# Value products of an attention in two halves of the head's dimension, on 64x32 instead of 64x64 tiles of the TensorE array

## Chip, cores and metric

The kernel runs on one core of one Trainium2 chip. The metric is the device time of one execution in microseconds (us). Three runs of the kernel before gave 911.26, 908.46 and 911.06 us; the median is 911.06 us. A measurement of this kernel can tell a difference from no change when it is over about 0.3%, which is 2.7 us.

## The reference

The reference is an attention followed by a feed-forward block, all in float32. For 8 batches and 8 heads of 576 positions with a head dimension of 64:

```python
scores = scale * np.matmul(q, k.transpose(0, 1, 3, 2))
rel = pos[:, None] - pos[None, :]
mask_plain = (rel >= 0) & (rel < 32)
mask_dil = (rel >= 0) & (rel < 128) & (rel % 4 == 0)
...
attn = np.exp(scores - np.max(scores, axis=-1, keepdims=True))
attn = attn / (np.sum(attn, axis=-1, keepdims=True) + 1e-09)
out = np.matmul(attn, v)
...
h = x @ w_in
sp = np.maximum(h, 0.0) + np.log1p(np.exp(-np.abs(h)))
y = (h * erf(sp)) @ w_out
```

Heads 0 to 3 use the plain mask, heads 4 to 7 the dilated one. `x` is the attention's output as a matrix of 4608 tokens by 512, `w_in` is 512x2048 and `w_out` 2048x512. The last matrix `y` is the result.

## The kernel before, in words

**The attention** works on units. The sequence is cut into strips of 32 queries (`STRIP`), and each strip looks at 64 keys (`KEYS`): its own 32 and the 32 before it. The dilated heads are put in an order in which the same holds. A unit is 8 strips (`SPU`) of two heads; there are 72 units (`NU`). A unit goes through these steps:

- `scores` (L221): 16 products on TensorE, for each strip and each of the two heads `h`. The stationary operand is 64 partitions (the head's dimension) by 32 queries, the moving one 64 partitions by 64 keys. Each runs on a tile of the array of 64 rows by 32 columns, at row 0 or 64 and at column 0, 32, 64 or 96, so that eight such tiles lie beside each other.
- `mask_max` on VectorE, `exponents` on ScalarE, `normalize` on VectorE and GpSimd.
- `transposes` (L260): two transposes of 128x128 on TensorE, and a copy `turned` (L264) of the result from PSUM into `pT`, which holds keys on partitions.
- `values` (L279): 16 products on TensorE, for each of 4 columns of strips `s`, the two halves `p` of the partitions and the two heads `h`. The stationary operand is the value tile `v`, 64 keys by the 64 of the head's dimension; the moving one is 64 keys by 32 queries of `pT`. Each runs on a tile of 64 rows by 64 columns, of which there are four. The result, 64 partitions by 32, lies in PSUM.
- `rows` (L321): ScalarE copies that PSUM out into a tile of rows, which later becomes the input of the feed-forward block.

The operands are plain float32, and such a product is carried out as two pairs of a weight load and a matmul. So the 1152 products of `values` show as 2304 weight loads and 2304 matmuls in the trace, and so do the 1152 of `scores`.

**The feed-forward block** splits its operands into a high and a low part and multiplies them in three products of 128x128 tiles (`mm1`, L528, `mm1_fast`, L649, and `mm2`, L702). These fill TensorE for most of the span.

**The order of the work** is written out by hand. The first 14 units are scored in `first_visit`, one visit each; in each visit from the fourth on, the unit of three visits before is transposed and gets its value products, with a few idle products (`busy`, L361) between. After that, a loop over half steps `x` of the feed-forward block takes up further visits at half steps that `visits` lists. In such a visit `attend` issues the value products of the units that are ready, and right behind them, on the same queue of TensorE, the scores of the units that are due:

```python
def attend(ready, scored):
    for u in ready:
        values(u)
    for u in scored:
        scores(u)
    for u in ready:
        rows(u)
```

Ten visits have one unit in each list. From then on a visit has two: 24 visits have two ready and two scored units, and the last two visits have only value products, of two units and of one. With the 11 visits of the beginning that makes 11 + 10 + 48 + 2 + 1 = 72 units.

The value products of a unit wait for its copied transposes and for the DMA that brought `v`; the scores wait for the DMA that brought `qk`.

Of the kernel before, what the change touches and what calls it, by code (L numbers as in the profile page):

```python
# [18 lines left out]
P = 128  # L19
B, H, S, D = 8, 8, 576, 64  # L20
# [5 lines left out]
STRIP = 32  # L26
NSTRIP = S // STRIP
KEYS = STRIP + WIN
# [111 lines left out]
def attn_moe_kernel(ctx: ExitStack, tc: tile.TileContext, qk, v, masks, eye, w_in, w_out, out):  # L140
    nc = tc.nc
# [43 lines left out]
    def place(u, p):  # L185


        if u < FREE:
            return acc[(u + 1 + 2 * p) % 4][:, p * P:(p + 1) * P]
        at = PARTS * P + (u in second) * P  # L190
        return spb[p][:, at:at + P]
# [80 lines left out]
    def values(u):  # L272
        vt, pt = vz[u % 2], pz[u in second]
        for s in range(SIDE):
            qs = slice(s * STRIP, (s + 1) * STRIP)
            for p in range(PARTS):
                ks, xp = slice(p * KEYS, (p + 1) * KEYS), place(u, p)
                for h in range(2):
                    nc.tensor.matmul(xp[h * D:(h + 1) * D, qs], vt[ks, s, h, :],  # L279
                                     pt[ks, h * P + s * STRIP:h * P + (s + 1) * STRIP], start=True, stop=True,  # L280
                                     tile_position=(p * KEYS, h * D))

    def attend(ready, scored):
        for u in ready:
# [5 lines that stand above are left out]
# [73 lines left out]
    def first_visit(n):  # L363

        m = n - LAG
        copy = nc.scalar.copy if n in EARLY else nc.vector.tensor_copy
        if has(m):
            transposes(m)
        scores(n)
        if n != DEEP - 3:  # L370
            load_qk(n + 3 if n < DEEP - 3 else n + 2)
        if n < 3:
            load_w(n)
        busy(2 if has(m) else 3)
        if has(m):
            turned(m, copy)
        if n in EARLY:
            prep_act()
        if has(m):
            values(m)  # L380
            busy(2)
        if has(n - 2):
            normalize(n - 2)
        mask_max(n)
        part_lo()
        if has(m):
            rows(m)
            finish(m)
        if m == NBLK - 1:
            part_lo()  # L390
        exponents(n)
        load_v(n - 1)
# [80 lines left out]
    h = ps.tile([P, TOK], F32, name="h")  # L473
# [3 lines left out]
    at = {0: [[x[:, i, 0:TOK] for x in xs] for i in range(2)]}  # L477
# [456 lines left out]
```

## Time and profile before

| | |
|---|---|
| median of three runs | 911.06 us (908.46 to 911.26) |
| span of the profiled execution (the page gives no other time of it) | 908.9 us |
| TensorE matmuls busy | 884.3 us, 97% of the span |
| weight loads busy | 753.5 us, 83% |
| VectorE, ScalarE, GpSimd busy | 669.6, 600.7 and 77.9 us |
| mean granted TensorE clock | 0.994 |
| chain of work that ended last | 85% TensorE, of it L279 and L221 about 3% each |

In the rows, PE is TensorE's matmul and PEld its weight load, which overlaps it; DVE is VectorE, ACT ScalarE, POOL GpSimd and SP SyncE. L279 is line 279 of the kernel before. A row of the timeline gives the start and the length of a merged group in us, from its first start to its last end, and its count. In a line's own view stand the shortest, median and longest duration of one instruction in ns, and the first and the last start in us. Matmuls are pipelined: many are under way at once, so the pace is read from their starts and not from their lengths.

### The profile page before, as it was taken

How to read it: one execution, taken by the hardware profiler on the slowest of the kernel's cores; microseconds unless marked ns; L12 is line 12 of the kernel's file. 1: busy time of each engine (PE TensorE's matmuls, PEld its weight loads, DVE VectorE, ACT ScalarE, POOL GpSimd, SP SyncE). 2: the span in 40 equal slices, each digit the busy share in tenths (PEclk: the TensorE clock that was granted, in tenths of full speed). 3: DMA queues.
4: the chain of work that ended last, by engine and by line, in shares of the span. 5: the costliest groups of instructions: out<-in, count | busy, mean ns of one | idle time of the engine just before them, and what ended most of it. 6: DMA issues, size and time to landing. Idle time of an engine off the chain costs nothing.

```text
span 908.9 us, 22857 instructions
## 1 busy us (share of the span) xinstructions
PE 884.3 (97%) x9129; PEld 753.5 (83%) x9129; DVE 669.6 (74%) x1702; ACT 600.7 (66%) x1267; POOL 77.9 (9%) x97
## 2 busy tenths in 40 slices
PE   7789999999999999999999999999999999999998
PEld 3367777888887888889989988888988999999996
DVE  3889879886688888668776777678666866776555
ACT  5889879876678687666776676669654644545442
POOL 2322100000011100000100000000000000000000
PEclk7999999999999999999999999999999999999999
DMA  8784444432458688687668765877567546655521
GB/s 276 250 273 149 137 159 135 136 127 80 150 199 324 232 284 309 241 284 227 219 206 283 262 213 191 289 266 252 185 237 230 185 146 230 233 180 203 199 84 47
DMA packets 69450, 188.89 MB, mean 208 GB/s; under 512 B 9184, under 2 KB 17632, under 8 KB 63200
## 3 DMA queue, kind: packets, MB, share of 16 engines
q1 hardware_dynamic: 69056, 186.91, 60.9%
q8 instruction: 72, 1.18, 0.5%
q10 hardware_dynamic: 288, 0.52, 0.1%
q14 instruction: 34, 0.28, 0.1%
HBM read 153.85 MB, written 33.55 MB: 206 GB/s over the span
## 4 chain that ended last, share of the span: by engine, by line
PE 85%; DVE 7%; DMA 3%; ACT 2%; issue 1%; POOL 1%; SPq 0%; DVEq 0%; POOLq 0%; ACTq 0%
PE acc L702 40%; PE h L649 15%; PE tx L649 12%; PE h L528 10%; PE sp L279 3%; PE sp L221 3%; PE sp L260 1%; DMA dbl<-in_w_in_dram 1%; DMA v<-in_v_dram 1%; DVE s L684 1%; DVE hc L670 1%; DVE w L465 1%; ACT prob L242 1%; DVE prob L232 1%; POOL prob L255 0%
## 5 line engine op out<-in xcount | busy, mean ns | idle before, releaser
L702 PE MATMUL acc<-wout_hi,ghi 128*128 128x512 f32 x576 | 228.4, 397 | 0.5 <-DVE ghi L687 0.4
L702 PE MATMUL acc<-wout_lo,ghi 128*128 128x512 f32 x576 | 225.7, 392 | 0.0
L674 ACT ACTIVATE s<-hc 128x1024 f32<-128x1024 f32 x72 | 76.5, 1062 | 189.4 <-DVE hc L663 171.2
L702 PE MATMUL acc<-wout_hi,glo 128*128 128x512 f32 x576 | 159.0, 389 | 0.0
L702 PEld LDWEIGHTS acc<-wout_hi,glo 128*128 128x128 f32 x576 | 108.1, 188 | 22.7
L702 PEld LDWEIGHTS acc<-wout_hi,ghi 128*128 128x128 f32 x576 | 108.6, 188 | 20.7 <-DVE ghi L687 0.9
L702 PEld LDWEIGHTS acc<-wout_lo,ghi 128*128 128x128 f32 x576 | 108.7, 189 | 19.5
L255 POOL TENSOR_TENSOR prob<-prob,rinv 128x256 f32<-128x256 f32 x72 | 69.0, 968 | 539.0 <-DVE ssum L253 314.1
L688 DVE TENSOR_TENSOR glo<-s,ghi 128x512 fp32r<-128x512 f32 x144 | 100.1, 695 | 5.5 <-PE acc L702 0.5
L242 ACT ACTIVATE prob<-prob,nmax 128x64 f32<-128x64 f32 x288 | 96.4, 338 | 7.6 <-DVE nmax L232 7.1
L684 DVE TENSOR_TENSOR s<-hc,s 128x1024 f32<-128x1024 f32 x72 | 92.9, 1290 | 9.2 <-ACT s L677 9.1
L528 PE MATMUL h<-x,win 128*128 128x512 f32 x384 | 96.6, 394 | 2.6 <-DVE hc L670 2.5
L649 PE MATMUL h<-win 128*128 128x256 f32 x720 | 98.1, 283 | 0.0
L674 ACT ACT_TABLE_LOAD x72 | 92.4, 1283 | 1.3
L677 ACT ACT_TABLE_LOAD x72 | 92.4, 1283 | 1.3
L649 PEld LDWEIGHTS h<-win 128*128 128x128 f32 x720 | 91.6, 192 | 0.0
L528 PEld LDWEIGHTS h<-x,win 128*128 128x128 f32 x384 | 71.2, 188 | 18.8 <-DVE hc L670 3.7
L677 ACT ACTIVATE s<-s 128x1024 f32<-128x1024 f32 x72 | 76.3, 1060 | 0.8
L232 DVE CUSTOM_DVE_ANT_0 prob<-sp,cst 128x64 f32<-128x64 f32 x288 | 45.4, 220 | 36.9 <-ACT rows L321 20.1
L687 DVE CAST ghi<-s 128x512 fp32r<-128x512 f32 x144 | 68.5, 475 | 3.1 <-PE acc L702 0.6
L321 ACT COPY rows<-sp 128x128 f32<-128x128 f32 (+7 forms) x167 | 27.9, 308 | 57.3 <-PE sp L221 55.0
L659 DVE TENSOR_TENSOR hc<-h,hc 128x512 f32<-128x512 f32 x48 | 33.2, 692 | 41.1 <-PE h L649 40.8
(110 smaller groups left out, 1257.6 us busy)
## 6 DMA issues: line engine op xcount, KB each, us to landing
win<-ws SPq DMA_DIRECT2D x48, 1024.0 KB, 5.5
win<-ws SPq DMA_DIRECT2D x48, 768.0 KB, 4.5
v<-in_v_dram SPq DMA_DIRECT2D x72, 256.0 KB, 4.1
qk<-in_qk_dram SPq DMA_DIRECT2D x45, 272.0 KB, 3.9
dbl<-in_w_in_dram SPq DMA_DIRECT2D x16, 512.0 KB, 4.0
dbl<-in_w_out_dram SPq DMA_DIRECT2D x16, 512.0 KB, 3.7
ws<-x SPq DMA_DIRECT2D x32, 256.0 KB, 4.1
xT<-rows SPq DMA_DIRECT2D x24, 288.0 KB, 5.0
```

The lines of the kernel that those rows point to most:

```text
L232: nc.vector.tensor_tensor_reduce(out=pr[:, g, :], in0=sps[h][:, u % 2, p, :], in1=mask[QUADS.index(kinds(u, p))], scale=-SCALE, scalar=BIG ...
L242: nc.scalar.activation(out=probs[u][:, j, :], in_=probs[u][:, j, :], func=AF.Exp, scale=-1.0, bias=nmax[:, j:j + 1], accum_out=sums[u][:, ...
L255: nc.gpsimd.tensor_tensor(probs[u], probs[u], rinv.broadcast_to([P, 2 * PARTS, KEYS]), op=ALU.mult)
L528: nc.tensor.matmul(h, win_at[:, ftp, j, cc // 2, w, cc % 2, :], x[cc], start=(k == 0 and i == 0), stop=(k == CC - 1 and i == 2))
L649: nc.tensor.matmul((h, bank)[b][:, half * HN:(half + 1) * HN], w[:, k, wi, c, :], x[:, xi, c, :], start=(c == 0 and n == 0), stop=(c == 1 ...
L659: nc.vector.tensor_tensor(out=a[:, 0:2], in0=x, in1=a[:, 2:3].broadcast_to([P, 2, HN]), op=ALU.add)
L674: nc.scalar.activation(out=ls[t], in_=hs[t], func=AF.Softplus)
L677: nc.scalar.activation(out=ls[t], in_=ls[t], func=AF.Erf)
L684: nc.vector.tensor_tensor(out=e, in0=hc, in1=e, op=ALU.mult)
L687: nc.vector.tensor_copy(out=ghi, in_=e[:, j])
L688: nc.vector.tensor_tensor(out=glo, in0=e[:, j], in1=ghi.bitcast(F32), op=ALU.subtract)
L702: nc.tensor.matmul(acc[tt], g[:, tt * P:(tt + 1) * P], w[:, ft, :], start=(first and w is wout_hi and g is ghi), stop=(last and g is glo))
```

## The change

Each value product of 64 keys by 64 of the head's dimension becomes two products of 64 keys by 32, one for each half of the dimension. Each half has the same moving operand as the whole had. Its tile of the array has 64 rows and 32 columns, and its result goes to the same 32 partitions of the same place in PSUM as that half of the result did before.

```diff
                 for h in range(2):
-                    nc.tensor.matmul(xp[h * D:(h + 1) * D, qs], vt[ks, s, h, :],
-                                     pt[ks, h * P + s * STRIP:h * P + (s + 1) * STRIP], start=True, stop=True,
-                                     tile_position=(p * KEYS, h * D))
+                    for d in range(0, D, STRIP):
+                        at = h * D + d
+                        nc.tensor.matmul(xp[at:at + STRIP, qs], vt[ks, s, h, d:d + STRIP],
+                                         pt[ks, h * P + s * STRIP:h * P + (s + 1) * STRIP], start=True, stop=True,
+                                         tile_position=(p * KEYS, at))
```

`values` now issues 32 products per unit instead of 16, or 64 pairs of a weight load and a matmul instead of 32. All else stays, the waits too. On TensorE's queue, this is the end of the first unit's value products and the beginning of the second's, and the beginning of the scores, in a visit of two units, before (`sp_90` and `sp_91` are the two PSUM banks, one for each half of the rows; `x2` counts equal neighbours; 64x32 is the result's shape):

```order
L279 MATMUL sp_90<-pT_88,v_87 64x32 x2
L279 MATMUL sp_91<-pT_88,v_87 64x32 x2
L279 MATMUL sp_90<-pT_89,v_86 64x32 [waits DMAHW1_49]
L279 MATMUL sp_90<-pT_89,v_86 64x32
...
L279 MATMUL sp_91<-pT_89,v_86 64x32 x2
L221 MATMUL sp_90<-qk_83 32x64 [waits DMAHW6_49]
L221 MATMUL sp_91<-qk_83 32x64
```

And the same place now:

```order
L281 MATMUL sp_90<-pT_88,v_87 32x32 x4
L281 MATMUL sp_91<-pT_88,v_87 32x32 x4
L281 MATMUL sp_90<-pT_89,v_86 32x32 [waits DMAHW1_49]
L281 MATMUL sp_90<-pT_89,v_86 32x32 x3
...
L281 MATMUL sp_91<-pT_89,v_86 32x32 x4
L221 MATMUL sp_90<-qk_83 32x64 [waits DMAHW6_49]
L221 MATMUL sp_91<-qk_83 32x64
```

Nothing has moved against its neighbours, and no wait has come or gone; each value product stands there twice, with half the result, and the tile of the array now has the shape that the scores behind it use. The queues of the other engines are the same as before.

## Prediction

> **What bounds the kernel now.** I read the page first, for the engine that sets the end.
>
> ```profile
> span 908.9 us, 22857 instructions
> PE 884.3 (97%) x9129; PEld 753.5 (83%) x9129; DVE 669.6 (74%) x1702; ACT 600.7 (66%) x1267; POOL 77.9 (9%) x97
> ...
> PE 85%; DVE 7%; DMA 3%; ACT 2%; issue 1%; POOL 1%; SPq 0%; DVEq 0%; POOLq 0%; ACTq 0%
> ```
>
> TensorE sets it. Next, busy time by stage: the first row below is the part of the first visits, the second holds over half of the 24 visits of two units.
>
> ```profile
> 0.00:54.00 54.00, 40.71 (x957) 21.98 (x957) 35.54 (x166) 39.95 (x175) 16.62 (x32) 0.91 0.79 255
> 350.00:690.00 340.00, 340.00 (x3952) 305.31 (x3946) 245.41 (x662) 227.79 (x498) 29.35 (x30) 1.00 0.71 242
> ```
>
> The first number behind the stretch's length is TensorE. In the long stage it has no idle time at all, so whatever a visit takes longer or shorter on its queue goes straight into the end. At the beginning it idles for 13.3 of 54 us, so most of what a visit takes there is hidden. Then the timeline, for one visit of two units, one of one unit, one of the beginning, and the two last with value products alone; between them the start of what follows.
>
> ```profile
> 298.89 1.14 PE L279 MATMUL sp<-pT,v 64*64 64x32 f32 x64
> 299.96 0.86 PE L221 MATMUL sp<-qk 64*32 64x64 f32 x64
> 300.74 0.50 PE L528 MATMUL h<-dbl,win 128*128 128x512 f32 x1
> ...
> 83.94 0.67 PE L279 MATMUL sp<-pT,v 64*64 64x32 f32 x32
> 84.54 0.45 PE L221 MATMUL sp<-qk 64*32 64x64 f32 x32
> 84.93 0.50 PE L528 MATMUL h<-x,win 128*128 128x512 f32 x1
> ...
> 48.99 0.67 PE L279 MATMUL acc<-pT,v 64*64 64x32 f32 x32
> 49.59 0.60 PE L361 MATMUL h<-plain 128*128 128x512 bf16 x2
> ...
> 660.56 1.14 PE L279 MATMUL sp<-pT,v 64*64 64x32 f32 x64
> 661.63 1.09 PE L649 MATMUL tx<-x,win 128*128 128x256 f32 x7
> ...
> 683.06 0.67 PE L279 MATMUL sp<-pT,v 64*64 64x32 f32 x32
> 683.66 0.61 PE L649 MATMUL tx<-x,win 128*128 128x256 f32 x3
> ```
>
> From first start to the start of what follows, a visit of two units takes 300.74 - 298.89 = 1.85 us, one of one unit 0.99 us, the value products alone 0.60 us for a unit and 1.07 us for two. Last, the two lines' own views, for the length of one instruction:
>
> ```profile
> L279 PEld LDWEIGHTS sp<-pT,v x1824: 129/135/135, 77.0 to 683.5; 64*64 64x64 f32 x183
> L279 PE MATMUL sp<-pT,v x1824: 219/219/242, 77.0 to 683.5; 64*64 64x32 f32 x183
> ...
> L221 PEld LDWEIGHTS sp<-qk x2144: 102/106/174, 3.6 to 649.2; 64*32 64x32 f32 x195
> L221 PE MATMUL sp<-qk x2144: 212/216/313, 3.6 to 649.3; 64*32 64x64 f32 x195
> ```
>
> **Pace and gaps.** A matmul of either line lasts about 0.22 us, so the last start is 0.22 us ahead of a group's end. The value products of two units have their last start at 298.89 + 1.14 - 0.22 = 299.81, and the scores begin at 299.96: a gap of 0.15 us, and likewise 0.14 us behind the scores (300.60 to 300.74). Both are places where the tile of the array changes its shape. For the pace I looked at narrow cuts of the same visit: weight loads amid the value products, amid the first unit's scores and late in the second unit's, and the matmuls of the second unit's scores.
>
> ```profile
> 299.18 0.56 PEld L279 LDWEIGHTS sp<-pT,v 64*64 64x64 f32 x31
> 300.00 0.24 PEld L221 LDWEIGHTS sp<-qk 64*32 64x32 f32 x22
> 300.33 0.32 PEld L221 LDWEIGHTS sp<-qk 64*32 64x32 f32 x26
> 300.22 0.59 PE L221 MATMUL sp<-qk 64*32 64x64 f32 x32
> ```
>
> Less one load's length and divided by the count less one, a pair starts every (560 - 135) / 30 = 14.2 ns in the value products, every (240 - 106) / 21 = 6.4 ns in the first unit's scores, and every (320 - 106) / 25 = 8.6 ns in the second unit's. The second unit's scores begin 300.22 - 299.96 = 0.26 us behind the first's, and their 32 starts take 0.59 - 0.22 = 0.37 us; at 8.6 ns they would take 0.27, so 0.10 us are lost near their beginning. In the visit of one unit the 32 starts of the scores take 0.45 - 0.22 = 0.23 us.
>
> I read this so: on 64x32 tiles the array can start a pair every 6.4 ns, but only for the first 32 or so, which have been waiting on TensorE's queue; then the queue has run dry, there is a pause of 0.10 us, and from there pairs come at 8.6 ns, as fast as they are brought up. On 64x64 tiles the array itself is slower (14.2 ns) than the supply, and nobody notices the supply.
>
> **The change part by part.** It adds 2304 pairs, 64 per visit of two units. Each has half the columns to load; the rows give 106 ns instead of 135 for such a load. It removes the change of shape between value products and scores.
>
> A visit of two units has now 64 value products and 32 scores on one shape, 96 products or 192 pairs in one run. Priced by the scores: the 33rd pair starts at 0.26 us, the pause is 0.10, the other 159 come at 8.6 ns or 1.37 us, and behind the last start stand 0.14 us up to the next line: 1.87 us, against 1.85. That is +0.02 us, 24 times: +0.5 us. The 0.15 us of the gap and the 29 ns per load are gained, and the 64 added pairs, 0.55 us at 8.6 ns, take them back.
>
> A visit of one unit has 96 pairs: 0.26 + 0.10 + 63 x 0.0086 + 0.14 = 1.04 us against 0.99, ten times +0.05: +0.5 us.
>
> The two last visits have value products alone: 128 pairs, 0.26 + 0.10 + 95 x 0.0086 + 0.15 = 1.33 against 1.07; and 64 pairs, 0.26 + 0.10 + 31 x 0.0086 + 0.15 = 0.78 against 0.60: +0.4 us together.
>
> In the first visits it is likewise 0.78 against 0.60, but only where the visit is on the chain. In order of time the chain has, of the eleven:
>
> ```profile
> 13.48 1.08 PE acc L279 x32
> 17.53 1.01 PE acc L279 x32
> 21.51 1.02 PE acc L279 x32
> ...
> 31.73 0.67 PE acc L279 x32
> ```
>
> The three of about 1.0 us run while the clock is still low (the stage has 0.91 on the mean, above). If the supply doesn't follow the array's clock, they shrink from about 1.0 to about 0.9: I take -0.1 us for each, between 0 and -0.2. The fourth loses 0.18. Sum: -0.1 us. The seven others are covered by the idle time above; without that cover they would cost 7 x 0.18 = 1.3 us.
>
> All together +0.5 + 0.5 + 0.4 - 0.1 = +1.3 us. The profiled execution's span is 908.9 us, 2.2 us under the median of the runs, which lies within their spread (908.46 to 911.26); the difference is put on the median: 911.06 + 1.3 = **912.4 us**. The other engines don't enter. Of them, ScalarE's copies wait longest for the end of a visit, as the scores' own view says:
>
> ```profile
>   ACT rows L321: 55.0, 24
> ```
>
> These are 2.3 us in each of the 24 visits, on an engine that is not on the chain, and the end of a visit moves by hundredths of a microsecond.
>
> No row shows one shape running on from one line to another, so the 0.15 us could stay: the unknown is bounded by 0 and 34 x 0.15 = 5.1 us. I take 0, since between the two units' value products, where the shape stays, no gap shows (1.07 us for two units is under twice 0.60). The Trainium skill, TensorEngine Tiling (Array Packing), section Key Properties, says that changing the tiling mode, not just the tile, drains the engine; the gaps agree with it, and by it the gap goes.
>
> **The rivals.** *The pace holds* (0.20). The pause in the scores stands where the second unit begins, at an instruction that waits for a DMA; it may belong to that and not to a queue run dry. Then value products run as the first unit's scores do, 7 ns a pair, with the scores behind them as now: 128 x 0.007 + 0.78 = 1.68 us, -0.17 in 24 visits; 64 x 0.007 + 0.39 = 0.84, -0.15 in ten; together -5.6 us, **905.4 us**. For it: the first 32 pairs of scores never falter in the rows above. Against it: the pace stays at 8.6 ns long after the pause.
>
> *Every unit's beginning pauses* (0.17, slower). The same instruction with its wait stands ahead of the second unit's value products and of each unit's scores. Today the one amid value products is covered, since 14.2 ns a pair leaves slack over 8.6. If the pause belongs to it, and the pace behind it is the supply's, a visit of two units has three such pauses instead of one: +0.20 us, 24 times +4.8, less what the first visits don't pay (0.2): 911.06 + 1.3 + 4.6 = **917.0 us**. It decides as soon as the array's pace falls under 8.6 ns. Against it: in the visit of one unit the scores begin with such an instruction too, and their 32 starts take 0.23 us, without a pause.
>
> *The gap stays* (0.10, slower). If the 0.15 us are the way of results into PSUM, and not the shape, it is +5.1 on the sum: **917.5 us**.
>
> *The added pairs simply come on top* (0.03, slower). If a load of 32 columns took as long as one of 64, the 128 pairs kept 14.2 ns by turns of four and nothing came back but the gap: 64 x 0.0086 - 0.15 = +0.40 us in 24 visits, +0.13 in ten, +0.8 at the end: about **923 us**. Against it: 106 against 135 ns.
>
> The Trainium skill speaks against the change: TensorEngine Tiling, section Instruction Overhead, gives each matmul about 60 cycles and advises not to take the tiling factor from a dimension that is already small. At the 2.4 GHz that the Trainium skill gives TensorE (TensorE: Matmul & The Clock Gate, its table of specifications), 60 cycles are 25 ns, and 2304 added pairs would cost 58 us by this estimate. The trace doesn't bear that price out: tiled pairs start every 6.4 to 14.2 ns.
>
> **How the numbers follow.** My forecast has 0.50. Within it the pace of 8.6 ns, read from rounded rows, may be 8.3 or 9.0: 192 pairs make 0.05 us a visit, 1.5 us in all, so it stays within 0.3% (2.7 us) with 0.42, is slower with 0.06 and faster with 0.02. Faster: 0.02 + 0.20 = 0.22. Same: 0.42. Slower: 0.06 + 0.17 + 0.10 + 0.03 = 0.36. The range takes in the first three rivals' values, 905 to 917.5 us; the forecast's own is 910.5 to 914.5.
>
> **What would show it.** In the changed profile a visit of two units should be one run of matmuls of both lines without a gap between them, about 1.87 us up to the next line, with pairs of value products every 6 to 7 ns in the first quarter of a microsecond, a pause of about 0.1, and 8.6 ns behind it; the visit of two units at the end should take 1.33 us. I am wrong if the value products keep 7 ns throughout (faster), if pauses stand at each unit's first product, if a gap of 0.15 us stays ahead of the scores, or if the pairs start every 14 ns as they do now.

## The result, and the profile after

Six runs of the kernel after gave a median of 941.96 us, beside 911.16 us for the kernel before on the same chips. One of the six, 999.12 us, had a mean granted clock of 0.842, against 0.981 to 0.991 in the others, and is left out of what follows. The median of the other five is 941.39 us and the ratio 1.033 (95% interval 1.031 to 1.035): 3.3% slower, 30.2 us, where 912.4 us had been forecast and 917.5 us was the upper end of the range.

The page of after: its first lines, the DMA queue that brings instructions, and the chain of work that ended last.

```profile
span 940.6 us, 27452 instructions
...
PE 896.5 (95%) x11420; PEld 764.8 (81%) x11433; DVE 669.4 (71%) x1702; ACT 600.9 (64%) x1267; POOL 77.6 (8%) x97
...
q8 instruction: 90, 1.47, 0.6%
...
PE 83%; DVE 7%; issue 4%; ACT 3%; DMA 2%; SPq 0%; POOL 0%; DVEq 0%; ACTq 0%; POOLq 0%
```

The same queue on the page of before:

```profile
q8 instruction: 72, 1.18, 0.5%
```

TensorE is busy 12.2 us longer, but the span grew by 31.7 us, so most of the loss is idle time on an engine that had next to none. On the chain "issue" went from 1% to 4%. That is time in which TensorE waits for nothing that the trace names. The waits of TensorE from 170 us on, the part with the visits of two units, show which lines stand behind these stretches of idle time, called holes from here on; first after, then before. The columns are the total in us, the number of waits, and the longest.

```profile
PE sp L221 <- issue: 16.2, 9, 3.4
PE tx L651 <- issue: 2.4, 2, 1.3
PE h L530 <- issue: 0.7, 1, 0.7
...
```

```profile
PE sp L260 <- POOL prob L255: 1.0, 3, 0.7
PE h L528 <- DVE hc L670: 0.7, 1, 0.7
PE sp L279 <- DVE pT L264: 0.5, 1, 0.5
```

The holes are in the scores, or just behind a visit, and in the scores' code nothing was changed. The timeline of three visits of two units in after, one without a hole, one with a hole, and one with a hole behind it:

```profile
588.35 1.26 PE L281 MATMUL sp<-pT,v 64*32 64x32 f32 x126
...
589.45 0.82 PE L221 MATMUL sp<-qk 64*32 64x64 f32 x62
590.20 1.70 PE L651 MATMUL tx<-win 128*128 128x256 f32 x12
...
611.88 1.26 PE L281 MATMUL sp<-pT,v 64*32 64x32 f32 x126
...
612.97 0.67 PE L221 MATMUL sp<-qk 64*32 64x64 f32 x45
615.95 0.52 PE L221 MATMUL sp<-qk 64*32 64x64 f32 x17 [2.31 <-issue]
616.40 1.86 PE L651 MATMUL tx<-win 128*128 128x256 f32 x7
...
563.24 1.26 PE L281 MATMUL sp<-pT,v 64*32 64x32 f32 x126
...
565.09 0.74 PE L651 MATMUL tx<-win 128*128 128x256 f32 x4
567.15 1.10 PE L651 MATMUL tx<-win 128*128 128x256 f32 x7 [1.32 <-issue]
```

The first goes just as forecast: 590.20 - 588.35 = 1.85 us up to the next line, one run without a gap. The second stops after 47 of the 64 matmuls of its scores and goes on 2.5 us later (start to start; the row counts from the modelled end of the matmul before). The third is whole and the products behind it stop.

**What the holes are.** The queue "instruction" brought 72 packets before and 90 after, 1.47 MB / 90 = 16.3 KB each. TensorE's stream, counted in the order of the program (a float32 product is two loads and two matmuls, so four; any other product and a transpose two; an instruction that only waits one), has 18,456 instructions before and 23,064 after: 72.1 and 90.1 times 256. So a packet is a block of 256 instructions. All 13 holes of the visits of two units stand where the count reaches the end of a block, always at the same remainder when it is divided by 256, 194. At the visit of 611.88 us a block ends 94 instructions behind the visit's start (at 612.27 us) and the next one ends 256 further on, at the 350th of its 384: there is the hole. The DMA view of that visit, from 611.9 to 615.9 us, in 40 slices of 0.1 us:

```profile
DMA  3924011100000800000000000977991188997429
...
q8 instruction: 1, 0.02, 2.0%
```

This view puts the whole time of a packet into the slice in which it begins. The instruction packet is the 8 in the fourteenth slice, at 613.2 us; 2.0% of 16 engines over 4.0 us are 1.3 us. I read it so: the next block is asked for when the previous one ends and TensorE enters the block in hand (612.27), its packet begins 0.97 us later, takes 1.3 us, and the first new instruction starts 1.4 us after that: 3.7 us. The block in hand, at 8.6 ns for a pair, was used up in 1.16 us. The difference is the hole of 2.5 us.

Not every visit has one. At the visit of 336.06 us a block ends 4 instructions behind the start, and the next 260 behind it. There was no hole, and the same view from 334 to 336 us shows why: the packet lay from 334.31 to 335.28 us and had come before the visit began. I take it that TensorE's queue had run ahead through the slow products.

```profile
q8 instruction: 1, 0.02, 3.0%
```

Over the 24 visits of two units of after: a hole wherever a block's end lies 29 to 143 instructions behind the visit's start, none at 4, 12, or 178 to 250.

**The clock.** Behind a hole the granted clock may drop as well. The windows around two holes, in the visits of 220.72 and 611.88 us: length, the busy time of TensorE (first the matmuls, then the loads) and of the other engines, then PEclk, DMA share and GB/s.

```profile
222.93:226.34 3.41, 1.80 (x37) 1.49 (x38) 0.36 (x5) 1.13 (x8) 0.00 (x0) 1.00 0.88 305
226.34:229.76 3.42, 3.42 (x17) 2.83 (x16) 2.60 (x17) 3.41 (x14) 0.00 (x0) 1.00 0.71 266
...
612.05:615.46 3.41, 1.60 (x175) 1.43 (x158) 0.42 (x1) 0.00 (x0) 0.00 (x0) 1.00 0.33 88
615.50:622.20 6.70, 6.25 (x43) 5.98 (x44) 1.94 (x18) 5.55 (x25) 0.00 (x0) 0.50 0.57 178
622.30:626.00 3.70, 3.70 (x23) 3.23 (x22) 2.12 (x5) 3.11 (x3) 0.00 (x0) 1.00 0.83 268
```

Behind the hole in the visit of 611.88 us TensorE runs at half its clock for 6.7 us, which costs some 2.5 us on top; behind that of 220.72 us, nearly as long (2.4 against 2.5 us), it keeps its clock. The clock fell with five of the six holes of 1.9 us or more, for 3.4 us in the four other cases, and with none of the shorter ones. What decides it is counted behind the experiments.

**The sum.** I matched the two traces visit by visit, from the start of one visit of two units to the start of the next. The first of them begins 0.8 us later than before (171.17 against 170.40). Holes in or right behind the visits: 22.5 us. The rest of the intervals, nearly all of it in the five with a halved clock: 8.1 us. The end, without its hole: 0.3 us. Together 31.7 us, the whole difference of the spans. In the 11 intervals without a hole after and before differ by 0.03 us at most.

### The profile page after: what moved, and what is told of

Its sections match the earlier page's. It is cut to its first block, busy times and chain, and to the rows that moved or that the text cites. A ratio compares the mean times of both kernels' runs of the same rounds, so it can differ in the third digit from the quotient of the medians.

```text
span 940.6 us, 27452 instructions
## 1 busy us (share of the span) xinstructions
PE 896.5 (95%) x11420; PEld 764.8 (81%) x11433; DVE 669.4 (71%) x1702; ACT 600.9 (64%) x1267; POOL 77.6 (8%) x97
## 3 DMA queue, kind: packets, MB, share of 16 engines
q8 instruction: 90, 1.47, 0.6%
## 4 chain that ended last, share of the span: by engine, by line
PE 83%; DVE 7%; issue 4%; ACT 3%; DMA 2%; SPq 0%; POOL 0%; DVEq 0%; ACTq 0%; POOLq 0%
PE acc L704 38%; PE h L651 15%; PE tx L651 12%; PE h L530 9%; PE sp L281 3%; PE sp L221 3%; PE sp L260 1%; DMA dbl<-in_w_in_dram 1%; PE h L363 1%; DVE s L686 1%; ACT prob L242 1%; PE acc L281 1%; DVE hc L672 1%; DVE w L467 1%; DVE win L462 0%
```

## The experiments

Theory F: the instruction blocks run out. Rival R: the holes belong to the half products themselves, or to what certain visits wait for (a late load of q, k or v). Rival T: a throttle after dense work.

### The stream moved by 64 and by 192 instructions

The kernel after, with 16 (or 48) small products at the start. They add 64 (or 192) instructions and nothing else.

```diff
         busy(4)
+        for k in range(16):
+            r = k % 4
+            nc.tensor.matmul(h[r * STRIP:(r + 1) * STRIP, 0:8], plain[0:D, 0:STRIP],
+                             plain[0:D, 0:8], start=True, stop=True,
+                             tile_position=(0, r * STRIP))
```

> The kernel after, with 16 small float32 products (64 instructions of TensorE's stream) at the very beginning, whose results nobody uses; all else is the same. Theory F (TensorE's instructions come by DMA in blocks of 256; a hole opens where a run of fast products takes up a whole block before the next has come): counted from the trace of after, a two-unit visit has its hole where a block ends between about 15 and 150 instructions behind its start. 64 instructions more move every such end 64 forward: holes now in the nine visits that began in after at 195.5, 362.1, 409.9, 471.2, 515.0, 563.2, 611.9, 640.7 and 653.7 us (six of which had none within the visit), and none any more in those of 220.7, 274.7, 289.1, 308.2, 385.9, 487.8, 538.5 and 677.2 us. The sum of the holes in the two-unit visits goes from about 21.6 to about 16 us, the time to 936 us (930 to 942; what the first visits do is not known to better than 4 us). Rival R (the holes belong to what certain visits wait for, a late load of q, k or v or the copied transposes, or to the half products themselves): the same eight visits and three others as in after have the holes, 942 us within 2. Rival T (a throttle that cuts in after so much dense work): holes at the same times, 942 us.

Measured: 937.52 us, ratio to before 1.031 (1.029 to 1.034). Two visits in the timeline, the one that began at 487.76 us in after (a hole of 2.3 us there) and the one that began at 514.98 us (none there):

```profile
481.16 1.26 PE L281 MATMUL sp<-pT,v 64*32 64x32 f32 x126
...
482.25 0.82 PE L221 MATMUL sp<-qk 64*32 64x64 f32 x62
483.01 0.86 PE L651 MATMUL tx<-x,win 128*128 128x256 f32 x5
...
504.69 1.25 PE L281 MATMUL sp<-pT,v 64*32 64x32 f32 x125
...
505.78 0.76 PE L221 MATMUL sp<-qk 64*32 64x64 f32 x55
508.72 0.31 PE L221 MATMUL sp<-qk 64*32 64x64 f32 x7 [2.18 <-issue]
```

The hole has gone from the one and come to the other. All nine visits named have one (1.6 to 4.0 us; at the visit named 640.7 it is behind the run), six of the eight others have lost theirs. Two not foreseen: at 289.1 us one of 1.3 us, where a block's end lies 248 behind the start, and at 308.2 us one of 0.3, where it lies 14 behind. The holes sum up to 22.1 us, hardly less than after's 22.5 and not the 16 expected: of the 6.7 us between the spans 3.7 lie ahead of the first visit of two units and 2.5 in fewer stretches of low clock. So the places speak for F; the time came out as expected for other reasons.

> As the run before, with 48 small products, so 192 instructions more at the beginning. Theory F: 16 visits have holes: those that began in after at 171.2, 220.7, 247.4, 260.9, 274.7, 289.1, 308.2, 336.1, 385.9, 434.6, 447.6, 471.2, 487.8, 538.5, 588.4 and 677.2 us; none at 195.5, 362.1, 409.9, 515.0, 563.2, 611.9, 640.7 and 653.7 us. Sum of the holes some 31 us against 21.6 us in after, so 951 us (945 to 958), 15 us more than with 64 instructions, though the work differs by 32 products of 8 columns. Rivals R and T: 942 us within 2, the holes where after has them.

Measured: 953.72 us, ratio 1.047 (1.045 to 1.049). All 16 visits named have a hole, in the run or right behind it; of the eight others seven have none, and one (611.9) a small one behind it, 0.5 us. Together 30.1 us. The waits of TensorE:

```profile
PE sp L221 <- issue: 21.6, 12, 2.3
PE acc L281 <- issue: 3.2, 3, 2.0
PE tx L651 <- issue: 2.0, 2, 1.3
```

Two kernels whose work differs by 32 tiny products are 16 us apart. R and T, by which the same visits keep their holes, fall.

### Before, with each score product issued twice

```diff
-                nc.tensor.matmul(sps[h][r * STRIP:(r + 1) * STRIP, i, p, :], z[hs, s * STRIP:(s + 1) * STRIP],
-                                 z[hs, at:at + KEYS], start=True, stop=True,
-                                 tile_position=(h * D, r * STRIP))
+                for _ in range(2):
+                    nc.tensor.matmul(sps[h][r * STRIP:(r + 1) * STRIP, i, p, :], z[hs, s * STRIP:(s + 1) * STRIP],
+                                     z[hs, at:at + KEYS], start=True, stop=True,
+                                     tile_position=(h * D, r * STRIP))
```

> The kernel before, whose value products are whole (64x64 tiles), with each score product issued twice over, to the same place and with the same result; nothing of the change is in it. A two-unit visit has 128 + 256 = 384 instructions, as many as in after. Without holes this costs 64 pairs at 8.6 ns in each of 24 visits (13 us), half of that in ten (3 us) and up to as much in the first ones (4 us): 927 to 931 us. Theory F: holes come although no value product was halved; since three units' scores more are issued ahead of each visit than in after, the stream stands 192 instructions further, so the holes are in the same 16 visits as in the run with 192 instructions, each shorter by up to 0.5 us as a block that holds whole value products lasts longer: 20 to 28 us in the two-unit visits, 955 us in all (946 to 965). Rival R in the form that the halves are at fault, and a rival by which 64x32 tiles are at fault only beside new weights: no holes, 929 us.

Measured: 958.31 us, ratio 1.0525 (1.051 to 1.054). One visit of it:

```profile
553.35 1.14 PE L280 MATMUL sp<-pT,v 64*64 64x32 f32 x64
554.42 1.62 PE L222 MATMUL sp<-qk 64*32 64x64 f32 x110
557.10 0.46 PE L222 MATMUL sp<-qk 64*32 64x64 f32 x18 [1.06 <-issue]
557.49 1.69 PE L650 MATMUL tx<-x,win 128*128 128x256 f32 x12
```

The holes are there without the change, in 14 of the 16 visits named and in no other. The doubled pairs, twice in a row on one tile, are slower than I had taken: a visit without a hole lasts 2.86 us, 1.0 and not 0.55 us more than before. Over 24 visits that is 24 us and over ten visits of one unit 6 us, so that 941 us and not 929 is the time without holes; the holes are smaller in return, 15.8 us in sum. The total is near by two errors that balance. It shows the size rule, though: in the twelve visits that have a hole inside the run both here and in the run with 192 instructions, it is 1.2 us here on the mean and 2.1 there. The visit lasts 1.0 us longer and the hole is 0.9 us shorter.

### The scores apart from the value products

```diff
                 weights(x)
+                for u in scored:
+                    scores(u)
                 mm2(t - 2, j)
...
             if t >= 2:
-                attend(ready, scored)
+                attend(ready, [])
```

> The kernel after, with the scores of a visit issued ahead of the second layer's products (mm2) of that half step and the value products behind them, so that 24 slow instructions lie between the two; the work is the same. The longest run is now 256 instructions instead of 384. Theory F: a whole block fits into a run hardly ever; holes stay only where a block ends within some 20 instructions behind a run, which by the count is at the visits that began in after at 195.5, 409.9 and 563.2 us (1.1 to 1.6 us each), and in the first visits, which are not touched (5 us). Two more changes of the tile's shape in each of 24 visits cost 0.15 to 0.3 us, so 4 to 7 us. In all 931 us (924 to 936). Rival R (the halves, their tiles or the loads): the holes stay, and the changes of shape come on top: 946 to 949 us.

Measured: 965.83 us, ratio 1.061 (1.059 to 1.0635), outside what either theory had. The waits of TensorE:

```profile
PE sp L221 <- DVE pT L264: 29.0, 30, 4.2
...
PE acc L281 <- issue: 3.0, 2, 2.2
...
PE sp L221 <- issue: 1.8, 1, 1.8
```

The waits for nothing are down from some 27 to 6 us, as F says, and a new wait of 29.0 us stands in their place: the scores now follow the transposes on the queue, write to the same bank of PSUM, and so wait until VectorE has copied the transposes out. The second layer's products, which used to cover that copy, are queued behind them. The next run but one puts the scores ahead of the transposes.

### Cut to fit, scores first, and two controls

In the first of these, a table of 24 numbers says how many instructions to add ahead of each visit of two units, so that no block ends in the wrong place; `cuts(x)` takes from it into how many pieces the next product is cut, one, two or rarely four:

```diff
-                    nc.tensor.matmul(acc[tt], g[:, tt * P:(tt + 1) * P], w[:, ft, :],
+                    n = 1 if first or last else cuts(x)
+                    for a in range(0, DM, DM // n):
+                        nc.tensor.matmul(acc[tt][:, a:a + DM // n], g[:, tt * P:(tt + 1) * P], w[:, ft, a:a + DM // n],
...
```

> The kernel after with all its work; only the products of the second layer (mm2) are cut, some 790 of 1728 of them into two products of 256 columns, which adds two instructions each. Where they are cut is so chosen by counting the stream that no visit of two units has a block's end between 14 and 158 instructions behind its start; in the traces of after and of the first two runs, 46 of the 47 visits with a hole have it there, and none of the visits with their end elsewhere but one has a hole. The first layer's products of 256 columns come every 120 ns, those of 512 every 227, so a cut costs about 13 ns, 10 us in all. Theory F: no hole (or one) in the 24 visits, and the rest as predicted before the result: 911.2 + 1.3 + 10 = 922 us (917 to 927), 20 us less than after though it has 1580 instructions more. Rivals by which the half products, their loads or a throttle are at fault: the holes stay and the cuts come on top, 950 us (946 to 956).

(The count in that text is wrong: 41 visits of the three traces have a hole, and 40 of them have a block's end 14 to 158 behind their start.) Measured: 929.5 us, ratio 1.021 (1.019 to 1.022), 12 us less than after with 1582 instructions more, and 2.5 us over the expected range. The waits of TensorE from 170 to 690 us hold one row of this kind, in place of the 19 us of after:

```profile
PE sp L221 <- issue: 2.8, 2, 1.5
```

Both holes, 1.5 and 1.7 us start to start, are in visits with the block's end 3 and 4 behind the start. I had called that safe. Their packets began 0.4 and 0.6 us behind the visit's start, not well ahead of it; cut products come every 120 ns, so the same number of queued instructions gives less time in advance. (That reason is argued from the two times and not tried.) The cuts cost more than thought: from each of the second layer's products to the start of what follows it is 405.3 us in sum, against 390.1 before, 15.2 us and not 10. A cut in two costs about what was expected, since halves of 256 columns start every 120 ns and a whole product takes 227. The 38 products that were cut in four cost 0.2 us each, since their quarters of 128 columns still start only every 111 ns. So 22 of the 24 visits have no hole, as the count said, and the repair costs more than half of what it saves.

Then the scores ahead of the transposes, with the value products behind the second layer's:

```diff
             if t >= 2:
+                for u in scored:
+                    scores(u)
                 turn(ready)
...
-                attend(ready, scored)
+                attend(ready, [])
```

> The kernel after, with the scores of a visit issued ahead of its transposes (in the run before they stood behind them and waited 29 us for the copies of the transposes, since these lie in the same bank of PSUM; that wait was not foreseen), the second layer's products next, and the value products behind those. The longest run is 256 instructions. Theory F: by the count a block ends 14 to 30 instructions behind a run in three visits, 0.5 to 1 us each; no other holes in the visits of two units. One border more between shapes in each of 24 visits costs 0.1 to 0.25 us (2 to 6 us), and value products alone take 1.245 us in halves against 1.065 whole (the visit of two units at the end of after and of before), 4.3 us: 920 us (916 to 926). A rival by which the half products or their loads make the holes: they stay, 940 us or more. A wait that takes the scores' place again: the same 29 us at another instruction, 940 us as well, but not as a wait for nothing that the trace shows.

Measured: 928.87 us, ratio 1.018 (1.016 to 1.021), above the expected 916 to 926. And the same edit in the kernel before:

> The kernel before, whole value products, with the scores moved as in the run with the scores first: what that order costs by itself. Both theories: one border more per visit, 914 to 917 us, no holes. The difference to the run with the scores first is then what the halves cost where nothing runs out: 4 to 7 us by theory F (0.18 us in each of 24 visits, and up to three short holes), 25 us or more if the halves themselves make the holes.

Measured: 914.11 us, ratio 1.0035 (1.002 to 1.005). So the order costs 3 us, as expected, and the halves in it 14.8 us, where F had 4 to 7 and R 25 or more: between the two. The waits for nothing of TensorE from 170 to 690 us in the run with halves; with whole products there is no such row.

```profile
PE sp L281 <- issue: 2.0, 3, 0.9
PE tx L651 <- issue: 1.0, 2, 0.8
PE acc L704 <- issue: 0.6, 1, 0.6
```

Visit by visit, the value products of two units take 1.25 us in halves and 1.06 whole in each of the 24 visits (4.5 us). Seven holes of 0.3 to 1.1 us (5.4 us start to start) stand where I had counted three, and one of my three is among them. Four of the others follow a block that began 35 to 92 instructions ahead of the value products, in the run of the scores: the 32 slow instructions between (the transposes and the second layer's) are too few to make a block last. 2.4 us lie ahead of the first visit of two units, and 2.0 us in the interval of one visit, where TensorE waited 2.3 us for q and k (1.9 us in the run with whole products) and its clock was halved behind that wait alone. So the long holes are gone, and my rule for the short ones, taken from runs of another length, counted too few.

Last, the kernel after with whole value products wherever a visit has two ready units. These are the 24 visits of two units and also the first of the two last ones, which the text below counts among the halves:

```diff
-                    for d in range(0, D, STRIP):
+                    n = D if u in pairs else STRIP
+                    for d in range(0, D, n):
                         at = h * D + d
...
             second.update(ready[1:])
+            pairs.update(ready if len(ready) > 1 else [])
```

> The kernel after with whole value products in the 24 visits of two units and halves everywhere else (the first visits, the ten of one unit, the last two): the change without the part in which the holes of over 2 us lie from 170 us on. Theory F: runs of 256 instructions that take 1.85 us and more, no holes from 170 us on; at that point after was only 0.8 us behind before in spite of 8 us of holes, since the first visits wait for other engines as well: 912 us (909 to 915). A rival by which half products anywhere (in the first visits, say, through what they shift later) cost most of it: 925 us or more.

Measured: 912.81 us, ratio 1.002 (1.001 to 1.003). From 170 us on TensorE has no wait for nothing, and the halves in the other 22 visits cost 1.8 us. So some 28 of the 30 us come from the halves in these 25 visits.

No version beats the kernel before: without holes a visit in halves takes the 1.85 us that it took whole, so there is nothing to win by mending them.

## Why the prediction was wrong

- **The visit of two units**: forecast 1.87 us; 1.85 in 13 of the 14 visits without a hole inside (the other 2.11, against 2.17 before). The gap of 0.15 us at the change of shape is gone, as taken. The one pause behind the first 32 pairs is there: the 33rd matmul starts 78 ns behind the 32nd, against 0.10 us forecast. The term of +0.5 us is 0.0.
- **One unit, and the end**: 1.00 to 1.03 us in eight of the ten visits of one unit against a forecast of 1.04 (1.28 and 1.70 in the two others); 1.25 and 0.69 us at the end against 1.33 and 0.78. Each forecast is a little too high.
- **The first visits**: forecast -0.1 us, measured +2.1 us at the first visit of one unit (55.26 against 53.12 us), holes included. At the first visit of two units +0.4 was forecast, with the visits of one unit, and +0.8 measured. Other engines are waited for in between, which may have covered the rest; no run separates it.
- **The step that failed**: "the 33rd pair starts at 0.26 us, the pause is 0.10, the other 159 come at 8.6 ns or 1.37 us". The pace was nearly right: these 159 take 1.46 us in the visit of 588.35 us. But the supply was not endless: they take 4.05 us in the visit of 611.88 us. I had read the pace from visits of 256 instructions, where pairs come "as fast as they are brought up", and carried it on to 384. But they are brought up in blocks of 256, and a block takes 3 to 5 us from the moment the one before ends to its first instruction, where nothing was fetched ahead. Whole value products at 14.2 ns a pair make a visit of 256 last 1.85 us, and no run before is long enough to hold a whole block at the fast pace. In halves, 384 instructions at 4.3 ns each hold a whole block, or nearly, wherever a block ends 14 to 158 instructions behind the start; in 10 of the 24 visits the hole is inside, in 3 right behind. So in the 24 visits, where +0.5 us had been put, there are 22.5 us of holes.
- **The rivals**: pace holds (905.4), each unit's beginning pauses (917.0), gap stays (917.5), pairs on top (923): the rows show none of them. None had the supply of instructions in it, though the row "q8 instruction: 72" stood on the page of before.
- **What held and made it worse**: "whatever a visit takes longer or shorter on its queue goes straight into the end". So the 22.5 us of holes did, and 8.1 us of halved clock with them, of which the prediction had nothing.

The Trainium skill, Runtime: NRT & Kernel Launch, section Instruction fetch mechanics, says that instructions come in blocks of 16 KiB, 256 instructions, fetched while the current block runs, and that the cost of a boundary is mostly hidden. The sizes agree with the trace (90 packets for 90.1 x 256 instructions). That the cost is hidden is true of before (no wait for nothing from 170 us on); in after 13 boundaries in or right behind the visits of two units cost 0.35 to 3.65 us each.

**When the clock falls.** The ten traces together show it. Their record of the granted clock changes only in steps of 3.41 us. From 60 to 900 us there are 19 steps behind which the clock fell to half, and TensorE's matmuls were idle for 1.67 to 3.26 us of each; in no other step at full clock were they idle for more than 1.71 us. So the border lies at about half a step. What TensorE waited for makes no difference: in 15 of the 19 it was instructions, in three the copied transposes (in the run with the scores apart), and in one q and k. The last stands in the runs with the scores first, with halves and then with whole products; the second number is the busy time of the matmuls, and the third from the end PEclk:

```profile
286.22:289.63 3.41, 1.32 (x68) 0.72 (x66) 1.69 (x5) 3.37 (x4) 0.61 (x1) 1.00 0.97 307
289.63:293.04 3.41, 3.41 (x14) 2.84 (x11) 2.59 (x6) 0.80 (x1) 1.35 (x1) 0.50 1.06 407
```

```profile
283.27:286.68 3.41, 1.70 (x71) 1.36 (x69) 1.84 (x7) 3.37 (x4) 0.61 (x1) 1.00 0.94 329
286.68:290.10 3.42, 3.42 (x75) 2.71 (x73) 3.25 (x7) 0.42 (x1) 1.42 (x1) 1.00 1.05 399
```

The long hole of the visit of 220.72 us lies across two steps and leaves 1.80 of 3.41 us busy in the second: the clock stays.

One thing stays open: why one fetch takes 3 us and another 5. At the longest hole (3.65 us, at 289.12) the packet began 2.7 us after the block before had ended, while the DMA engines were full with other transfers (busy for 80% or more of each slice from 289 to 292 us); no run took that load away.

## What to carry to other kernels

An edit that adds instructions to a stretch where they are already issued as fast as they can be has a second price: count the stream in blocks of 256, look for the shortest time in which a run uses up a whole block, and compare it with the 3 to 5 us that the next block takes here. The row of the instruction queue and "issue" on the chain of waits are where it shows. Where such holes are in play, the time depends on where the blocks end, and an edit far ahead moved it by 16 us here: compare kernels by their visits without a hole first, and then count the holes.

## What the runs showed of the hardware

- TensorE asks for its next block of instructions when it enters the block in hand, as the packets of after lie at the 13 holes: they begin 0.5 to 2.7 us after that moment (up to 0.9 us ahead of it at three of the shorter holes), take 0.9 to 1.5 us, and the first instruction starts 1.2 to 1.6 us after their end.
- In a run of float32 pairs on 64x32 tiles the first 32 start every 6 to 7 ns, a pause of 78 ns follows, and from there a pair starts every 8.6 to 9.2 ns. That is about 4.3 to 4.6 ns an instruction, so a block lasts 1.1 to 1.2 us.
- Where the value products and the scores run on one shape of tile, the gap of 0.15 us between them is gone.
- The second layer's products start every 227 ns with 512 columns, every 120 ns with 256 and every 111 ns with 128: a cut in two costs 13 ns and a cut in four 0.2 us.
- The granted clock changes in steps of 3.41 us and fell to half behind steps in which TensorE was idle for about half of the time or more (1.67 us at the least), whatever it waited for.
